# Clustered attention and two MLPs on one core: centroids by one transfer, and the inputs of two later head pairs loaded ahead

## The chip, the core and the metric

The kernel runs on one core of a Trainium2 chip. A core has a matrix engine (TensorE, PE in the views, with its weight loads PEld), three engines for elementwise work (VectorE, DVE; ScalarE, ACT; GpSimd, POOL) and a queue engine (SyncE, SP) that issues most transfers; ACT can issue transfers too. Each engine works through its own list in order and waits for the others by semaphores. Data lies in HBM, is moved by 16 DMA engines into on-chip memory (SBUF), and matmuls write to PSUM, of which a bank holds 512 numbers in each of 128 partitions. The metric is the time of one execution on the device in microseconds (us); three runs are compared by their median.

## The reference

```python
q_n = q / (norm(q) + 1e-6); k_n = k / (norm(k) + 1e-6); c_n = centroids / (norm(centroids) + 1e-6)
q_assign = argmax(q_n @ c_n.T); k_assign = argmax(k_n @ c_n.T)          # one of 16 clusters per head
scores = where(q_assign == k_assign, q @ k.T / sqrt(64), -1e9)
attn = softmax(scores); x = attn @ v                                    # B 2, heads 8, S 768, D 64
h = x @ w_in;  x = (h * sigmoid(h)) @ w_out                             # 512 -> 2048 -> 512
out = (sigmoid(x @ w_gate) * (x @ w_val)) @ w_out2                      # 512 -> 1536 -> 512
```

Only the centroids' norms change an argmax over clusters, so the kernel scales the products with a centroid by the inverse of its norm (`unit`) and leaves the norms of q and k out.

## The kernel before

Two heads make a pair, 128 partitions high (`L` is the lower half, `U` the upper); there are 8 pairs, numbered from 0. The attention runs over the pairs, each with 12 tiles of 128 queries (6 for each head, `j` 0 and 1), and then the two MLPs follow with results in `acc`, a tile of 128 x 4 x 2 x 2 x 384 numbers in SBUF that holds the attention's result: `acc[:, hp, half, b]` belongs to the pair `hp` of batch `b` and is written when that pair is finished. Before that it lies idle.

For a pair, `load` brings `qq` and `kk` (128 x 768, 384 KB each), `load_values` brings `vv`. `prep` makes what the scores need: each operand is split in a rounded part (`qh`, `kh`) and the rest (`ql`, `kl`); transfers within SBUF put `qh` and `ql` on top of each other in `qa`, and `kh` twice in `ka`; `qm` and `km` (tiles `q` and `k` in the views) hold further parts, and 16 rows each that say which cluster a query or key chose, so that the matmul itself adds the mask.

The choice of clusters: `product_of_clusters` (L157, tile `pm`, matmuls of `qq` and `kk` with the centroids `cc`), `scaled` (L277, ACT, by `unit`, into `sim`), `similarities` (L168, three transposes into `ps`), a copy back (L64), and then on VectorE the maximum (`mx` for pair 0, `mk` later), equality (`eq`), rank (`wq`), its maximum, and the one-hot rows (`oh`). Transposes (`pt`) bring these to rows, which ACT and VectorE write into `q` and `k` for pair 0; for later pairs ACT writes `rows` and four small transfers carry them.

For a tile, `scores` (L468) does four matmuls into `s`, VectorE takes the maximum `nm` (L476), ACT the exponential `e` (L481); `s` has two buffers. `transposes` turns `e` (tiles `t` and `u`), copies `ph` on ACT or VectorE, and `values` (L518) multiplies by `vv` into `v`.

Set-up (L186 to L370) and the first two tiles are written out by hand for all engines but POOL. SP loads `cr` (the centroids as rows, 128 KB; L192), then `qq` and `kk` of pair 0; ACT loads the transposed centroids into `cc` in two parts (L196), whose other places VectorE has cleared. VectorE squares and sums `cr` (L263, L266), ACT takes the root (L268), VectorE forms `unit` (L269 to L274). `warm(n)` is n matmuls on zeros that fill TensorE's idle time: 10 at the start, 1 behind `pm`, 8 behind `ps`, 5 behind the second score tile. After that TensorE's order is fixed by `one_tile`: the scores of the tile two ahead, then the transposes of the present one, and pieces of `prep` of the next pair between, by a table (PIECES). VectorE, ACT, POOL and SP follow there in an order that a planner sets from this program order. Pair 1 is loaded behind the set-up's transfers (L615), pair 2 near the end of pair 0 (L656), later pairs in the middle of the pair two before. `pm` of pairs 1 and 2 is made within `prep`, that of later pairs a pair ahead.

Of the kernel before, what the change touches and what calls it, by code (L numbers as in the profile page):

```python
# [10 lines left out]
F32 = mybir.dt.float32  # L11
# [16 lines left out]
WARM = (10, 1, 8, 5)  # L28
# [3 lines left out]
def clustered_attention_then_two_mlps(ctx, tc, qT, kT, v, cen, cenT, w1i, w1o, w2g, w2v, w2o, out):  # L32
    nc = tc.nc
# [4 lines left out]
    P = 128  # L38
# [70 lines left out]
    with ExitStack() as att:  # L109
# [23 lines left out]
        def load(p):  # L133
            b, hp = divmod(p, HP)
            qq = raw.tile([P, S], F32, tag="qq", name=f"qq{p}")
            kk = raw.tile([P, S], F32, tag="kk", name=f"kk{p}")
            with after_masks(1) if p == 2 else nullcontext():
                nc.sync.dma_start(qq, qT[b, hp])
                nc.sync.dma_start(kk, kT[b, hp])
            raws[p] = (qq, kk)  # L140
# [49 lines left out]
        act_dma = nc.scalar.dma_start  # L190
        cr = cp.tile([P, HP, D], F32, tag="cr", name="cr")
        dma(cr, cen)  # L192
        cc = cp.tile([P, HP, 2, C], F32, tag="cc", name="cc")
        nc.vector.memset(cc, 0.0)
        for j, r in enumerate((L, U)):
            act_dma(cc[r, :, j], cenT[j])  # L196
# [4 lines left out]
        dma(kk, kT[0, 0])  # L201


        wt = fin.tile([P, S], F32, tag="rb", name="wt").bitcast(BF16)[:, 0:512]
        nc.vector.memset(wt, 0.0)
        pw = ps_v.tile([P, 512], F32, tag="v", name="pw")
# [54 lines left out]

        csq = cp.tile([P, HP, D], F32, tag="csq", name="csq")
# [26 lines left out]
        for j, (r, o) in enumerate(((L, U), (U, L))):  # L289
# [3 lines left out]
            dma(qa[o, j].bitcast(F32), ql[r].bitcast(F32))  # L293
            if j:
                dma(qm[r, j].bitcast(F32), qh[r].bitcast(F32))
        dma(vv, v[0, 0])
# [85 lines left out]

        def prep(p):
# [43 lines left out]
            sg = sim.rearrange("p t n j c -> p (t n j) c")  # L427
# [777 lines left out]
```

## Time and profile before

| | |
|---|---|
| median of 3 runs | 771.74 us (771.61 to 771.96) |
| profiled execution, span from first to last instruction | 770.1 us |
| TensorE busy | 760.9 us, 99% |
| VectorE busy | 620.1 us, 81% |
| ACT busy | 403.4 us, 52% |
| POOL busy | 393.8 us, 51% |
| bytes moved by DMA | 71.61 MB |

The page states no other time for the profiled execution than its span; the runs lie 1.6 us above it. The busy shares are means over the whole span, and say little of the first 15 us, which the change is about. A stretch there is read from the timeline: each line is an instruction or several alike, with its start, how long it ran, and in brackets how long its engine stood idle before it and what ended the wait.

### The profile page before, as it was taken

The numbers are of one execution on the slowest core, as the hardware profiler recorded it, in microseconds if no ns is written. First come the engines' busy times: TensorE is split into PE (matmuls) and PEld (weight loads), VectorE is DVE, ScalarE is ACT, GpSimd is POOL, SyncE is SP. The second block draws the span as 40 slices with busy tenths as digits, with TensorE's granted clock in tenths as the row PEclk, the third lists the DMA queues.
The fourth block names the chain that finished last, engine by engine and source line by source line (L and its number), as shares of the span: only waits on it lengthen the run. The fifth ranks groups of instructions, "written<-read, shape, count | busy, mean of one in ns | idle before, by whom it ended". The sixth has DMA issues, their size and how long they took to land.

```text
span 770.1 us, 11463 instructions
## 1 busy us (share of the span) xinstructions
PE 760.9 (99%) x4314; PEld 652.6 (85%) x4314; DVE 620.1 (81%) x787; ACT 403.4 (52%) x691; POOL 393.8 (51%) x345
## 2 busy tenths in 40 slices
PE   8999999999999999999999999999999999999998
PEld 4766777677768998998989989998998989899896
DVE  6887887788787968798978669996596997979645
ACT  6777776777886672543524516546442425344120
POOL 5235134643655773476646525644573937748320
PEclk9999999999999999999999999999999999999999
DMA  7677457447122122132222111221111221121004
GB/s 207 167 210 194 113 147 195 120 125 201 32 76 83 55 82 85 53 110 82 89 77 83 55 54 60 93 69 56 40 70 55 83 83 55 55 83 55 1 0 164
DMA packets 25488, 71.61 MB, mean 93 GB/s; under 512 B 4484, under 2 KB 4952, under 8 KB 25432
## 3 DMA queue, kind: packets, MB, share of 16 engines
q1 hardware_dynamic: 24888, 70.84, 31.1%
q8 instruction: 34, 0.56, 0.3%
q14 instruction: 22, 0.18, 0.1%
q10 hardware_dynamic: 544, 0.03, 0.0%
HBM read 48.01 MB, written 3.19 MB: 66 GB/s over the span
## 4 chain that ended last, share of the span: by engine, by line
PE 92%; DVE 3%; ACT 2%; DMA 1%; issue 1%; POOL 0%; SPq 0%; ACTq 0%
PE z L1021 13%; PE s L468 8%; PE v L518 7%; PE t L505 5%; PE y L962 4%; PE h_0w L846 4%; PE h_0x L846 4%; PE g_0w L846 3%; PE g_0x L846 3%; PE v_0w L846 3%; PE v_0x L846 3%; PE r L912 2%; PE q L912 2%; PE y_00None L962 2%; PE y_20None L962 2%; PE y_11None L962 2%
## 5 line engine op out<-in xcount | busy, mean ns | idle before, releaser
L481 ACT ACTIVATE e<-s,nm 128x768 f32<-128x768 f32 x96 | 86.5, 901 | 33.8 <-DVE nm L476 32.7
L476 DVE TENSOR_REDUCE nm<-s 128x1 f32<-128x768 f32 x96 | 91.4, 953 | 10.3 <-PE s L468 8.6
L1021 PE MATMUL z<-wu,ghb 128*128 128x512 f32 (+1 forms) x292 | 89.5, 388 | 0.0
L518 PE MATMUL v<-ph,vv 128*64 128x384 f32 x384 | 69.0, 494 | 0.2 <-DVE xf L530 0.2
L1021 PEld LDWEIGHTS z<-wu,ghb 128*128 128x128 f32 x292 | 54.2, 188 | 11.7 <-ACT ghb L64 0.6
L468 PE MATMUL s<-ka,qa 128*128 128x384 f32 x192 | 57.5, 380 | 1.7 <-ACT e L481 1.3
L505 PE MATMUL t<-ident,e 128*128 128x128 f32 x384 | 58.4, 275 | 0.1
L1021 PE MATMUL z<-wu,glb 128*128 128x512 f32 (+1 forms) x146 | 56.9, 390 | 0.0
L505 PEld LDWEIGHTS t<-ident,e 128*128 128x128 f32 x384 | 44.9, 140 | 11.3 <-issue 9.0
L518 PEld LDWEIGHTS v<-ph,vv 128*64 128x64 f32 x384 | 24.7, 136 | 32.8 <-issue 29.0
L468 PE MATMUL s<-k,q 128*128 128x384 f32 x192 | 49.7, 339 | 0.0
L942 DVE TENSOR_TENSOR acc<-z,acc 128x1024 f32<-128x1024 f32 (+2 forms) x32 | 36.6, 1152 | 13.8 <-PE z L1021 13.2
L64 ACT ACTIVATE ph<-t 128x512 f32<-128x512 f32 x68 | 40.6, 598 | 12.4 <-PE t L505 11.9
L67 DVE COPY ph<-u 128x512 f32<-128x512 f32 x48 | 32.8, 682 | 16.3 <-PE u L495 16.3
L549 POOL TENSOR_TENSOR acc<-xf,rb 128x768 f32<-128x768 f32 x7 | 12.9, 1837 | 58.5 <-DMA rb<-d_rb 40.0
L741 POOL TENSOR_TENSOR wo<-co,wo 128x512 fp32r<-128x512 f32 x16 | 23.5, 1471 | 33.6 <-ACT wo L64 33.6
L468 PEld LDWEIGHTS s<-k,q 128*128 128x128 f32 x192 | 34.5, 188 | 0.5 <-ACT k L338 0.3
L468 PEld LDWEIGHTS s<-ka,qa 128*128 128x128 f32 x192 | 28.9, 190 | 6.9 <-ACT e L481 6.0
L1021 PEld LDWEIGHTS z<-wu,glb 128*128 128x128 f32 x146 | 27.4, 188 | 6.9 <-DVE glb L902 1.4
L962 PE MATMUL y<-gha,wo 128*128 128x384 f32 x128 | 32.8, 334 | 0.0
L530 DVE TENSOR_TENSOR xf<-v,other 64x384 f32<-64x384 f32 x32 | 17.7, 553 | 14.8 <-ACT other L527 14.3
L395 POOL TENSOR_SCALAR qq<-qq 128x768 f32<-128x768 f32 x7 | 5.9, 838 | 38.2 <-PE pm L157 22.3
(629 smaller groups left out, 2160.3 us busy)
## 6 DMA issues: line engine op xcount, KB each, us to landing
ri<-in_w1i SPq DMA_DIRECT2D x16, 512.0 KB, 3.2
ro<-in_w1o SPq DMA_DIRECT2D x16, 512.0 KB, 3.2
ka<-kh SPq DMA_DIRECT2D x32, 192.0 KB, 3.4
rg<-in_w2g SPq DMA_DIRECT2D x12, 512.0 KB, 3.2
rv<-in_w2v SPq DMA_DIRECT2D x12, 512.0 KB, 3.2
ru<-in_w2o SPq DMA_DIRECT2D x12, 512.0 KB, 3.2
qq<-in_qT SPq DMA_DIRECT2D x8, 384.0 KB, 3.7
kk<-in_kT SPq DMA_DIRECT2D x8, 384.0 KB, 4.3
```

Of the source, the lines that this page charges most:

```text
L64: return nc.scalar.activation(o, i, AF.Copy)
L67: return nc.vector.tensor_copy(o, i)
L468: nc.tensor.matmul(s[:, g, 0:HS], lhsT=a[:, j, i * P : (i + 1) * P], rhs=c[:, j, g * HS : (g + 1) * HS], start=n == 0, stop=n == 1,)
L476: maxima.append(nc.vector.tensor_reduce(nm, s[:, :, 0:HS], axis=AX.XY, op=ALU.max, negate=True))
L481: x = nc.scalar.activation(e, s[:, :, 0:HS], AF.Exp, bias=nm, scale=1.0, accum_out=tots[p][:, n : n + 1])
L505: nc.tensor.transpose(t[:, kt, :], e[:, kt * P : (kt + 1) * P], ident)
L518: m = nc.tensor.matmul(o[(L, U)[kt % 2]], lhsT=vv[:, j, kt, :], rhs=ring[:, kt, g * G : (g + 1) * G], start=n < 2, stop=n >= NT - 2,)
L846: nc.tensor.matmul(o[:, b, 0:HS], lhsT=w[a][s][:, k, :], rhs=right[b, q][t][:, k, :], start=start and k == 0 and n == 0, stop=k == KQ - 1 ...
L912: nc.tensor.matmul(o[:, h, 0:HS], lhsT=w[f"a{m + 1}{r + 1}"][s][:, k, :], rhs=right[b, f"{r + 1}{h + 1}"][t][:, k, :], start=r == 0 and k ...
L942: added.append(nc.vector.tensor_tensor(z, o, z, op=ALU.add))
L962: nc.tensor.matmul(o[:, d, 0:width], lhsT=s[:, d, k, :], rhs=t[:, c], start=k == 0 and m == 0, stop=k == 1 and m == 2,)
L1021: nc.tensor.matmul(o[:, a, c], lhsT=s[:, q * P : (q + 1) * P], rhs=r[:, c], start=k == 0 and m == 0, stop=k == 1 and m == 2, skip_group_ch ...
```

## The change

The centroids. The transposed centroids come by one transfer to a tile `cs`, which two copies on VectorE bring to their places in `cc`; `cr` is loaded by ACT's queue behind it and no longer by SP's.

The loads. `qq` and `kk` of pairs 1 and 2 go into parts of `acc` that are written last in the first half of the attention. SP issues pair 1's right behind those of pair 0, and pair 2's behind the first four operand transfers, of which the last, `qa<-ql`, is now two of half the size. So `raw` gets pair 3 next.

The products. `pm` of pair 1 is made in the set-up behind `ps` of pair 0, and `pm` of pair 2 behind the second score tile, where `ps` of pair 1 now stands as well. Their scaled products lie in `acc` too. The fillers there go from 8 and 5 to 4 and 0.

```diff
-WARM = (10, 1, 8, 5)
+WARM = (10, 1, 4, 0)
+EARLY = (1, 2)
...
         act_dma = nc.scalar.dma_start
+        cs = cp.tile([P, HP, C], F32, tag="cs", name="cs")
+        act_dma(cs, cenT.rearrange("j d h c -> (j d) h c"))
         cr = cp.tile([P, HP, D], F32, tag="cr", name="cr")
-        dma(cr, cen)
+        act_dma(cr, cen)
         cc = cp.tile([P, HP, 2, C], F32, tag="cc", name="cc")
         nc.vector.memset(cc, 0.0)
-        for j, r in enumerate((L, U)):
-            act_dma(cc[r, :, j], cenT[j])
...
         dma(qq, qT[0, 0])
         dma(kk, kT[0, 0])
-
+        for p in EARLY:
+            raws[p] = tuple(acc[:, HP - p, n].rearrange("p b s -> p (b s)") for n in range(2))
+
+        def load_early(p):
+            for t, a in zip(raws[p], (qT, kT)):
+                dma(t, a[divmod(p, HP)])
+
+        load_early(EARLY[0])
...
+        for j, r in enumerate((L, U)):
+            nc.vector.tensor_copy(cc[r, :, j], cs[r])
         csq = cp.tile([P, HP, D], F32, tag="csq", name="csq")
         nc.vector.tensor_tensor(csq, cr, cr, op=ALU.mult)
...
-            dma(qa[o, j].bitcast(F32), ql[r].bitcast(F32))
+            for c in (slice(0, HS), slice(HS, S)) if j == 0 else (slice(0, S),):
+                dma(qa[o, j, c].bitcast(F32), ql[r, c].bitcast(F32))
             if j:
                 dma(qm[r, j].bitcast(F32), qh[r].bitcast(F32))
+            else:
+                load_early(EARLY[1])
         dma(vv, v[0, 0])
...
         similarities(ps, sums)
+        early = {EARLY[0]: ps_v.tile([P, 512], F32, tag="v", name=f"pm{EARLY[0]}")}
+        product_of_clusters(early[EARLY[0]], EARLY[0], *raws[EARLY[0]])
         warm(WARM[2])
...
         query_rows(0, pts[1], 0, half, half)
+        first_products = {p: acc[:, 0, n, B - 1, :] for n, p in enumerate(EARLY)}
+        scaled(EARLY[0], first_products[EARLY[0]], early[EARLY[0]][:, 0:HS])
...
-            sim = first_products.pop(p)
-            sums = sim.rearrange("p t n j c -> p (t n j c)")
-            yield
-            ps = ps_t.tile([P, 512], F32, tag="t", name=f"ps{p}")
-            similarities(ps, sums)
-            cast(nc.scalar, sums, ps[:, 0:HS])
+            sums = first_products.pop(p)
+            yield
+            if p != EARLY[0]:
+                seen(p, sums, nc.scalar)
...
-        if NPAIR > 1:
-            load(1)
-            load_values(1)
+        load_values(1)
         tiles = [(p, j, i) for p in range(NPAIR) for j in range(2) for i in range(NT)]
         for t in tiles[:2]:
             scores(*t)
+        seen(EARLY[0], first_products[EARLY[0]], nc.vector)
+        late_bank = ps_v.tile([P, 512], F32, tag="v", name=f"pm{EARLY[1]}")
+        product_of_clusters(late_bank, EARLY[1], *raws[EARLY[1]])
+        scaled(EARLY[1], first_products[EARLY[1]], late_bank[:, 0:HS])
         warm(WARM[3])
...
                 pieces(99)
-                if p == 0:
-                    load(p + 2)
                 if p + 2 < NPAIR:
                     load_values(p + 2)
```

`seen` is `similarities` and the copy back, as before. How the lists of the engines change is shown at two places.

The first is the start. SP's list before, from its first transfer (numbers in the names tell buffers apart):

```order
L192 DMA cr_105<-in_cen 128x256
L200 DMA qq0_111<-in_qT 128x768
L201 DMA kk0_112<-in_kT 128x768
L290 DMA qa0_194<-qh0_196 64x768
L291 DMA ka0_195<-kh0_198 64x768
L292 DMA ka0_195<-kh0_198 64x768
L293 DMA qa0_194<-ql0_197 64x768
L290 DMA qa0_194<-qh0_196 64x768
```

and now:

```order
L200 DMA qq0_111<-in_qT 128x768
L201 DMA kk0_112<-in_kT 128x768
L207 DMA acc_58<-in_qT 128x768
L207 DMA acc_58<-in_kT 128x768
L299 DMA qa0_198<-qh0_200 64x768
L300 DMA ka0_199<-kh0_202 64x768
L301 DMA ka0_199<-kh0_202 64x768
L303 DMA qa0_198<-ql0_201 64x384 x2
L207 DMA acc_58<-in_qT 128x768
L207 DMA acc_58<-in_kT 128x768
L299 DMA qa0_198<-qh0_200 64x768
```

ACT's list before, from its first transfer:

```order
L196 DMA cc_107<-in_cenT 64x4x16 x2
L229 ACT_TABLE_LOAD
L229 ACTIVATE sq_135<-sq_135 128x1
L267 ACTIVATE identb_134<-ident_129 128x128
L268 ACTIVATE r1_179<-r0_178 128x4
L284 ACTIVATE qh0_196<-qq0_111 128x768
L64 ACTIVATE kh0_198<-kk0_112 128x768
L277 ACTIVATE sim0_219<-pm0_213,unit_184 128x384
```

and now:

```order
L192 DMA cs_105<-in_cenT 128x64
L194 DMA cr_107<-in_cen 128x256
L236 ACT_TABLE_LOAD
L236 ACTIVATE sq_137<-sq_137 128x1
L276 ACTIVATE identb_136<-ident_131 128x128
L277 ACTIVATE r1_183<-r0_182 128x4
L293 ACTIVATE qh0_200<-qq0_111 128x768
L65 ACTIVATE kh0_202<-kk0_112 128x768
L286 ACTIVATE sim0_226<-pm0_220,unit_188 128x384
```

SP has lost `cr` and has two loads of pair 1 (into `acc`) ahead of the first operand transfer and two of pair 2 behind the fourth. ACT issues `cr` second; the root `r1<-r0`, which needs the sum of the squares of `cr`, stands ahead of `qh` as before.

The second place lies behind the first two score tiles. TensorE's list before, from the second tile to the transposes of the first:

```order
L468 MATMUL s0_0_1_283<-ka0_195,qa0_194 128x384 x2
L468 MATMUL s0_0_1_283<-k2_0_140,q2_0_138 128x384 x2
L210 LDWEIGHTS wt_116
L210 MATMUL pw_118<-wt_116 128x512
...
L468 MATMUL s0_0_2_305<-ka0_195,qa0_194 128x384 x2
L468 MATMUL s0_0_2_305<-k2_0_140,q2_0_138 128x384 x2
L505 MATMUL t0_0_0_320<-ident_129,e0_0_0_280 128x128 x4
```

and now:

```order
L486 MATMUL s0_0_1_288<-ka0_199,qa0_198 128x384 x2
L486 MATMUL s0_0_1_288<-k2_0_142,q2_0_140 128x384 x2
L168 MATMUL ps1_297<-ident_131,acc_58 128x128 x3
L157 MATMUL pm2_302<-acc_58,cc_109 32x384 x4
L486 MATMUL s0_0_2_316<-ka0_199,qa0_198 128x384 x2
L486 MATMUL s0_0_2_316<-k2_0_142,q2_0_140 128x384 x2
L523 MATMUL t0_0_0_331<-ident_131,e0_0_0_285 128x128 x4
L530 MATMUL u0_0_0_337<-ident_131,e0_0_0_285 128x128 x2
```

VectorE's list before, from the maximum of the second tile to that of the fifth:

```order
L476 TENSOR_REDUCE nm0_0_1_288<-s0_0_1_283 128x1
L173 TENSOR_REDUCE mx0_1_314<-sim0_219 128x12
L176 TENSOR_TENSOR eq0_1_316<-sim0_219,mx0_1_314 128x192
L178 TENSOR_TENSOR wq0_1_318<-eq0_1_316,rank_157 128x192
L476 TENSOR_REDUCE nm0_0_2_310<-s0_0_2_305 128x1
L181 TENSOR_REDUCE mw0_1_356<-wq0_1_318 128x12
L317 TENSOR_TENSOR oh_0_142<-wq0_1_318,mw0_1_356 128x6x16
L476 TENSOR_REDUCE nm0_0_3_334<-s0_0_3_329 128x1
L317 TENSOR_TENSOR oh_0_142<-wq0_1_318,mw0_1_356 128x6x16
L67 COPY ph_266<-u0_0_0_326 128x2x256
L67 COPY ph_266<-t0_0_1_341 128x4x128
L476 TENSOR_REDUCE nm0_0_4_352<-s0_0_4_347 128x1
```

and now:

```order
L68 COPY acc_58<-ps1_297 128x384
L176 TENSOR_TENSOR eq0_1_327<-sim0_226,mx0_1_325 128x192
L494 TENSOR_REDUCE nm0_0_2_321<-s0_0_2_316 128x1
L178 TENSOR_TENSOR wq0_1_329<-eq0_1_327,rank_159 128x192
L181 TENSOR_REDUCE mw0_1_367<-wq0_1_329 128x12
L494 TENSOR_REDUCE nm0_0_3_345<-s0_0_3_340 128x1
L68 COPY ph_275<-u0_0_0_337 128x2x256
L331 TENSOR_TENSOR oh_0_144<-wq0_1_329,mw0_1_367 128x6x16 x2
L68 COPY ph_275<-t0_0_1_352 128x4x128
L494 TENSOR_REDUCE nm0_0_4_363<-s0_0_4_358 128x1
L353 CAST k2_0_142<-pt0_1_371 16x768
L494 TENSOR_REDUCE nm0_0_5_404<-s0_0_5_399 128x1
```

TensorE has the three transposes of pair 1 and the product of pair 2 where five fillers were (one is shown). VectorE has the copy `acc<-ps1` ahead of the third tile's maximum, the step `wq0_1` behind it, and both `oh` steps behind a copy `ph`. Behind this place TensorE's list has no `pm` and no `ps` of pair 1 and no `pm` of pair 2 any more, and is otherwise as before.

## Rows read from the trace of the kernel before

**Rows 1.** Chain of waits, 0 to 70 us: start us, us, what it went through.

```profile
1.64 4.34 DMA kk<-in_kT
...
8.10 3.34 DMA qa<-ql
...
42.57 0.85 PE pm L157 x8
```

**Rows 2.** Timeline, ACT, first 14 us: start, us, instruction, tiles, idle before.

```profile
1.02 1.28 ACTq L196 DMA_DIRECT2D cc<-in_cenT  x2
...
3.94 0.19 ACT L268 ACTIVATE r<-r 128x4 f32<-128x4 f32 x1
4.86 0.84 ACT L284 ACTIVATE qh<-qq 128x768 fp32r<-128x768 f32 x1 [0.73 <-DMA qq<-in_qT]
6.00 0.84 ACT L64 ACTIVATE kh<-kk 128x768 fp32r<-128x768 f32 x1 [0.30 <-DMA kk<-in_kT]
7.22 0.58 ACT L277 ACTIVATE sim<-pm,unit 128x384 f32<-128x384 f32 x1 [0.38 <-PE pm L157]
...
12.19 0.74 ACT L328 ACTIVATE q<-pt 16x256 fp32r<-16x256 bf16 x2
```

**Rows 3.** Timeline, VectorE, set-up.

```profile
2.82 0.43 DVE L263 TENSOR_TENSOR csq<-cr 128x256 f32<-128x256 f32 x1 [0.69 <-DMA cr<-in_cen]
3.28 0.42 DVE L266 TENSOR_REDUCE r<-csq 128x4 f32<-128x256 f32 x1
...
5.18 0.18 DVE L274 RECIPROCAL unit<-r 128x4 f32<-128x4 f32 x1
5.73 0.96 DVE L285 SCALAR_TENSOR_TENSOR ql<-qq,qh 128x768 fp32r<-128x768 f32 x1 [0.38 <-ACT qh L284]
6.88 0.95 DVE L287 TENSOR_TENSOR k<-kk,kh 64x768 fp32r<-64x768 f32 x1 [0.18 <-ACT kh L64]
8.50 0.36 DVE L173 TENSOR_REDUCE mx<-ps 128x12 f32<-128x192 f32 x1 [0.67 <-PE ps L168]
```

**Rows 4.** Timeline, TensorE and its weight loads, set-up and first tiles.

```profile
6.28 0.48 PE L157 MATMUL pm<-qq,cc 128*32 128x384 f32 x1 [0.52 <-DMA cc<-in_cenT]
...
8.30 1.89 PE L210 MATMUL pw<-wt 128*128 128x512 bf16 x8
...
12.22 0.19 PEld L468 LDWEIGHTS s<-k,q 128*128 128x128 f32 x1 [0.26 <-ACT k L338]
...
12.85 0.51 PE L468 MATMUL s<-k,q 128*128 128x384 f32 x2
...
14.74 0.62 PE L468 MATMUL s<-ka,qa 128*128 128x384 f32 x2 [0.28 <-ACT e L481]
```

**Rows 5.** Stretches: us, busy of PE, PEld, DVE, ACT, POOL; PEclk, DMA share, GB/s.

```profile
3.00:5.00 2.00, 2.00 (x6) 0.76 (x5) 1.36 (x7) 1.26 (x5) 0.60 (x1) 1.00 0.99 340
15.75:24.39 8.64, 8.52 (x65) 6.75 (x64) 8.54 (x13) 7.21 (x15) 6.30 (x7) 1.00 0.74 221
24.98:33.36 8.38, 7.88 (x56) 5.46 (x58) 8.31 (x13) 6.19 (x12) 0.39 (x1) 1.00 0.90 210
36.00:62.00 26.00, 25.95 (x176) 17.79 (x174) 21.68 (x32) 18.62 (x37) 8.71 (x7) 1.00 0.71 189
```

**Rows 6.** Timeline, VectorE, the eighth tile's maximum.

```profile
24.98 0.96 DVE L476 TENSOR_REDUCE nm<-s 128x1 f32<-128x768 f32 x1 [0.59 <-PE s L468]
```

**Rows 7.** Timeline, SP's queue, its first two transfers.

```profile
0.73 0.39 SPq L192 DMA_DIRECT2D cr<-in_cen  x1
1.17 0.42 SPq L200 DMA_DIRECT2D qq<-in_qT  x1
```

**Rows 8.** DMA queues, 1.5 to 3.6 us: packets, MB, share of engines.

```profile
q1 hardware_dynamic: 245, 0.44, 80.3%
```

**Rows 9.** DMA queues, 4.6 to 5.7 us: q1 is SP's, q10 ACT's.

```profile
q1 hardware_dynamic: 53, 0.11, 26.3%
q10 hardware_dynamic: 283, 0.02, 17.5%
```

More of the change, by code (lines that the diff above doesn't have):

```diff
@@ L136, in load @@
             kk = raw.tile([P, S], F32, tag="kk", name=f"kk{p}")
-            with after_masks(1) if p == 2 else nullcontext():
-                nc.sync.dma_start(qq, qT[b, hp])
-                nc.sync.dma_start(kk, kT[b, hp])
+            nc.sync.dma_start(qq, qT[b, hp])
+            nc.sync.dma_start(kk, kT[b, hp])
             raws[p] = (qq, kk)
@@ L201, in clustered_attention_then_two_mlps @@
         dma(kk, kT[0, 0])
+        for p in EARLY:
[4 more added lines that the diff above has]
+        load_early(EARLY[0])
         wt = fin.tile([P, S], F32, tag="rb", name="wt").bitcast(BF16)[:, 0:512]
         nc.vector.memset(wt, 0.0)
-        pw = ps_v.tile([P, 512], F32, tag="v", name="pw")
+        pw = ps_s.tile([P, 512], F32, tag="s", name="pw")
         def warm(n):
@@ L370, in clustered_attention_then_two_mlps, with seen @@
         query_rows(0, pts[1], 0, half, half)
+        first_products = {p: acc[:, 0, n, B - 1, :] for n, p in enumerate(EARLY)}
+        scaled(EARLY[0], first_products[EARLY[0]], early[EARLY[0]][:, 0:HS])
         on_pool = {}
-        first_products = {}
         def clusters(p):
-            sim = wk.tile([P, NT, 2, 2, C], F32, tag="sim", name=f"sim{p}", bufs=1)
+            sim = wk.tile([P, HS], F32, tag="sim", name=f"sim{p}", bufs=1)
             pm = ps_t.tile([P, 512], F32, tag="t", name=f"pm{p}")
             product_of_clusters(pm, p, *raws[p][:2])
-            scaled(p, sim.rearrange("p t n j c -> p (t n j c)"), pm[:, 0:HS])
+            scaled(p, sim, pm[:, 0:HS])
             first_products[p] = sim
+        def seen(p, sums, eng):
+            ps = ps_t.tile([P, 512], F32, tag="t", name=f"ps{p}")
+            similarities(ps, sums)
+            cast(eng, sums, ps[:, 0:HS])
         def prep(p):
@@ L426, in prep @@
             W = 4 * NT
-            sg = sim.rearrange("p t n j c -> p (t n j) c")
+            sg = sums.rearrange("p (w c) -> p w c", c=C)
             queued(one, nc.vector.tensor_reduce, mk[:, 0, :], sg, axis=AX.X, op=ALU.max)
```

## The prediction

> **What bounds the kernel now.** I read the chain of waits from its start, then the timeline of each engine up to the first scores, the DMA queues in short stretches, and last the busy time by stretches. The reader should look for three things.
>
> First, the set-up is a chain, not a busy engine. The first keys land at 5.98 (1.64 + 4.34), and the copy of the low query half that the first scores need lands at 11.44 (8.10 + 3.34) [rows 1]. Close beside runs a second path, the choice of clusters: ACT turns pair 0 to `qh` and `kh` (4.86, 6.00) and scales the cluster product (`sim`, 7.22) [rows 2], VectorE picks the maximum (`mx`, 8.50) [rows 3]. The first score tile waits for both: the copy is there at 11.44, and the weights of the tile's last product wait 0.26 us for ACT's key rows `k`, the end of the choice [rows 4]. So the choice ends last; what delays it delays all that follows.
>
> Second, in the attention's first pair VectorE is the bound, although TensorE reads as busy: from 15.75 to 24.39 VectorE works 8.54 of 8.64 us, then after 0.59 us of waiting 8.31 of 8.38 us from 24.98 to 33.36 [rows 5, 6]. Third, from 36 to 62 TensorE works 25.95 of 26.00 us and VectorE only 21.68 [rows 5]: there a matmul that goes is time that goes.
>
> All sums are made against the profiled execution, whose span is 770.1 us. The timed runs (771.74) lie 1.6 us above it; that rest outside the span is taken as unchanged. Between changes of less than 0.2% (1.5 us) a measurement of this kernel does not tell.
>
> **The change part by part.**
>
> *Centroid rows `cr` to ACT's queue.* This is the term with the most in it. Now `cr` is SP's first transfer, issued at 0.73 [rows 7], and VectorE starts on it (`csq`) at 2.82 [rows 3]. After the change it is the second transfer on ACT's queue, the place that the second half of `cc` has now. ACT issues its two from 1.02 to 2.30 [rows 2]. In the queues' rows the ACT queue (q10) has no packet at all from 1.5 to 3.6 us; its second batch runs in 4.6 to 5.7, where SP's queue (q1) has only its last 53 packets left [rows 8, 9]. TensorE waits for `cc` until 6.28 [rows 4], 0.3 us after the keys. So what ACT asks for second comes when SP's second load is through, though it was asked for at nearly the same time. In the new order SP's second load is still `kk`. It is issued 0.44 us earlier, since `qq` starts at 0.73 instead of 1.17 [rows 7], so `kk` lands near 5.54. `cr` is 128 KB; at the 340 GB/s of the stretch 3.0 to 5.0 [rows 5] it takes 0.38 us more on engines that finish `kk` before that. I take 5.6 for the start of `csq`, with 3.5 (2.1 us after an issue near 1.5, as `cr` took alone) and 7.9 (behind the two new loads, 768 KB at 340 GB/s) as ends; 5.6 is by far nearest to the row of `cc`.
>
> The Trainium skill, in "DMA: Bandwidth & Descriptors" (Anatomy of one DMA), counts about 2.0 us fixed plus the bytes at 436 GB/s; by that `cr` would land near 4.0 and the set-up would lose nothing. The 2.06 us of `cr` alone on SP agree with it; the 4.6 us of `cc`'s second half do not.
>
> What hangs on `cr`: `csq` to the end of its sum 0.88 us, ACT's root `r` 0.19 and two hand-overs 0.07, the short steps to `unit` 1.23 (4.13 to 5.36), then in VectorE's order `ql` 0.96 and `k` 0.95, then `mx` [rows 2, 3]: 4.2 to 4.3 us from `csq` to `mx`. With 5.6 that is `mx` at 9.9 instead of 8.50. ACT says the same: the root stands ahead of `qh` in its order, so `qh` starts at 6.7 instead of 4.86, `kh` 0.84 later, `sim` at 8.4 instead of 7.22. With `csq` at 4.3 the term is nothing, before that a gain (rival A). **Set-up: +1.3 us.**
>
> *Centroids by one transfer, then two copies on VectorE.* Two requests become one, of 32 KB; the copies stand before `csq` and cost a few tenths that lie in its wait for `cr`. That `pm` no longer waits for `cc` is worth nothing, since `sim` behind it now waits for `kh` and `unit`.
>
> *Loads of pair 1 ahead.* 768 KB between `kk` and the copies. They take 2.3 us of DMA from 5.6 on, to 7.9; the first copy can't be asked for before `qh` is done, at 7.5. They hide in the delay of `cr`. If `cr` came early, they would lie in front of the copies, whose landing (now 11.44) would stay near 11, helped by the split of `qa<-ql` in two, of which the first score needs one. The product of pair 1 on TensorE stands where 8 of the filling matmuls (1.89 us at 8.30) and idle time are [rows 4]: nothing.
>
> *Products between the first scores.* After the second score tile (12.85 + 0.51) TensorE now fills, waits and starts the third tile at 14.74 [rows 4]. There stand instead `ps` of pair 1 (0.33), which needs ACT's scaling of 0.58 behind the query rows that end at 12.93 [rows 2], and `pm` of pair 2 (0.85): 13.5 + 0.4 + 0.85 = 14.8, so the third tile is 0.1 late. Pair 2's loads would land about 15 on a clock where this place has moved by 1.3 to 15.4; no wait, but with only 0.4 us of room. On VectorE the new cast (0.5) takes the gap before the third maximum, and one step `wq` (0.3) slips behind it, into the dense stretch. So that stretch ends 0.4 later, 24.8 instead of 24.39, against the next maximum at 24.98 now [rows 6]. TensorE loses `pm` and `ps` of pair 1 here, about 1.2 us, but VectorE lets through only 0.2. **Pair 0: -0.2 us.**
>
> *Pair 1.* `pm` of pair 2 goes from a stretch where TensorE is never idle: 0.85 us in the chain [rows 1]. ACT's scaling behind it goes as well; what is next there is the maximum of the tile before, ready 0.1 to 0.2 earlier. VectorE has 4.3 us of room in 26 [rows 5], so the whole 0.85 should pass; bounds 0 and 1.1. **Pair 1: -0.85 us.** Other pairs keep their order on TensorE and VectorE: nothing.
>
> Sum: +1.3 - 0.2 - 0.85 = +0.25, taken as +0.2: span 770.3, time 771.9.
>
> **The rivals.**
>
> *A, `cr` comes early.* If the DMA engines take ACT's requests in turn with SP's as soon as they are there, `cr` lands by 4. Then the earlier `qq` and `kk` show, up to 0.6 us at `mx` (`kk` 0.44 and the wait for `cc` 0.3, less the hand-over), and the gains stand: -0.6 - 0.2 - 0.85, and up to 0.2 more in pair 0: 769.9. For it: requests of 1 KB per partition instead of 64 bytes. Against it: no packet of ACT's queue before 3.6 [rows 8]. The Trainium skill ("DMA: Bandwidth & Descriptors", Queues, rings and completion order) has each DMA engine go round the queues packet by packet, which would bring `cr` in this way; the empty stretch in q10's rows does not show it.
>
> *B, `cr` falls behind the new loads too.* ACT's second request now ends at 2.30; SP would have asked for both loads of pair 1 by 2.6. If the order is by the time at which a request is complete, a slower issue on ACT puts one load (at 2.1) or both ahead of `cr`. With both, `csq` starts at 7.9, `mx` at 12.1, +3.6 - 1.05 = +2.5: 774.2. It decides from an end of ACT's issue later than 2.5. Against it: two-dimensional requests of 128 partitions take SP 0.39 to 0.43 [rows 7], by which ACT would end near 1.9.
>
> *C, pair 1 gives nothing*, because the maximum or the exponential of the neighbouring tile ends last once `pm` is gone: +1.3 - 0.2, 772.8. For it: `pm` is followed in the chain by ACT; against it VectorE's room.
>
> *D, the clock.* The fillers fall from 8 and 5 to 4 and 0, and TensorE will stand still longer in the set-up. The granted clock is 1.00 in every row [rows 5]; no row shows it fall. At its lower level, half, a few microseconds of matmuls would double: about 775.
>
> **How the numbers follow.** Forecast 0.57, its own range 771.2 to 772.6 (`cr` landing between 5.0 and 6.2); A 0.21, B 0.09, C 0.08, D 0.05. Faster: A and the edge of the forecast, 0.23. Slower: B and D and little else, 0.15. Same: 0.62. The range 769.7 to 773.5 leaves out B, D and the best of A.
>
> **What would show it.** `csq` waiting for `cr` until 5 to 6 us, `qh` starting right after `r` and not after its load, `mx` near 9.9; q10 empty until `qq` is through; VectorE without gaps from the third maximum to the eighth; no `pm` in pair 1 and about 0.85 less from there on. Wrong would be `csq` before 4.5, a wait of TensorE at `pm` of pair 2 for its load, a granted clock below 1.00, or a gain or loss that arises behind pair 1.

## The result: 0.9% slower, and the profile after

| | before | after |
|---|---|---|
| median of 5 runs each | 771.74 us (771.39 to 771.96) | 778.92 us (778.25 to 779.07) |
| span of the profiled execution | 770.1 us | 777.0 us |
| ratio of the times, 95% interval | | 1.009 (1.0078 to 1.0102) |

The forecast was 771.9, no change, with a range up to 773.5. The whole loss arises in the first pair of heads. The starts of VectorE's maxima `nm` in the two timelines, tile by tile from 0, show where (after minus before, us; tiles 0 to 11 belong to pair 0, 12 to 23 to pair 1):

| tile | 0 | 2 | 3 | 4 | 5 | 6 | 7 | 8 | 9 | 11 | 14 | 15 | 17 | 95 |
|---|---|---|---|---|---|---|---|---|---|---|---|---|---|---|
| | +1.29 | +2.43 | +2.54 | +5.68 | +6.86 | +6.87 | +6.36 | +6.86 | +7.72 | +7.20 | +7.49 | +6.56 | +6.92 | +6.66 |

So there are six steps: the set-up (+1.29), something ahead of tile 2 (+1.14), something ahead of tile 4 (+3.1), something ahead of tile 5 (+1.2), something ahead of tiles 8 and 9 (+1.4 together), and in pair 1 a gain at tile 15 (-0.93) between smaller losses (0.3 at tile 13, 0.4 at tile 17). The large ones are found in the timeline.

*Set-up.* VectorE and ACT of the kernel after, where [rows 2] and [rows 3] stood:

```profile
5.42 0.43 DVE L272 TENSOR_TENSOR csq<-cr 128x256 f32<-128x256 f32 x1 [0.99 <-DMA cr<-in_cen]
...
9.42 0.34 DVE L173 TENSOR_REDUCE mx<-ps 128x12 f32<-128x192 f32 x1
...
10.19 0.77 DVE L178 TENSOR_TENSOR wq<-eq,rank 128x192 bf16<-128x192 bf16 x1
```

```profile
6.34 0.20 ACT L277 ACTIVATE r<-r 128x4 f32<-128x4 f32 x1 [3.00 <-DVE r L275]
6.45 0.83 ACT L293 ACTIVATE qh<-qq 128x768 fp32r<-128x768 f32 x1
```

`cr` lands at 5.4 and ACT waits 3.00 us for the sum behind it. `mx` comes at 9.42 instead of 8.50. The step `wq` takes 0.77 us; before, the same step took 0.26 (at 9.28).

*Ahead of tile 2.* The chain of waits of the kernel after (start, us, what):

```profile
1.16 4.24 DMA cr<-in_cen
...
11.33 5.04 DMA acc<-in_kT
...
16.41 0.85 PE pm L157 x6
```

and TensorE's timeline there and behind:

```profile
15.36 0.83 PE L157 MATMUL pm<-acc,cc 128*32 128x384 f32 x2
16.41 0.85 PE L157 MATMUL pm<-acc,cc 128*32 128x384 f32 x6 [0.21 <-DMA acc<-in_kT]
17.18 0.61 PE L486 MATMUL s<-ka,qa 128*128 128x384 f32 x2
...
24.62 0.85 PE L339 MATMUL pt<-identb,oh 128*64 128x128 bf16 x6 [3.44 <-DVE oh L331]
```

The product of pair 2 waits for its second load, asked for at 11.33 and landed at 16.4. The row's idle time is only 0.21 us because two of the product's matmuls ran ahead of the load; the other six start 1.05 us behind them. The third score tile starts at 17.18 instead of 14.74 [rows 4]. Later TensorE stands still for 3.44 us, for the one-hot step `oh`.

*Ahead of tile 4.* VectorE's two `oh` steps and GpSimd at the same time:

```profile
21.18 1.61 DVE L331 TENSOR_TENSOR oh<-wq,mw 128x96 bf16<-128x96 bf16 x1
...
22.72 1.85 DVE L331 TENSOR_TENSOR oh<-wq,mw 128x96 bf16<-128x96 bf16 x1
```

```profile
20.87 1.81 POOL L420 TENSOR_TENSOR kl<-acc,kh 128x768 fp32r<-128x768 f32 x1
22.64 1.81 POOL L417 TENSOR_TENSOR ql<-acc,qh 128x768 fp32r<-128x768 f32 x1
```

Before, the two steps and the start of GpSimd's subtractions were these:

```profile
17.00 0.26 DVE L317 TENSOR_TENSOR oh<-wq,mw 128x96 bf16<-128x96 bf16 x1
...
18.05 0.25 DVE L317 TENSOR_TENSOR oh<-wq,mw 128x96 bf16<-128x96 bf16 x1
```

```profile
21.75 1.83 POOL L400 TENSOR_TENSOR kl<-kk,kh 128x768 fp32r<-128x768 f32 x1
```

Now the first ends at 22.79, 0.11 us behind the end of GpSimd's `kl` (22.68), the second at 24.57, 0.12 behind the end of `ql` (24.45). These are VectorE instructions with two operands in SBUF; before, they were over when the subtractions of pair 1 began. The `wq` of the set-up is the same: it ends at 10.96, GpSimd's scaling `acc<-acc` (10.02, 0.83) at 10.85.

*Ahead of tile 5.* The stretches, with the columns of [rows 5]:

```profile
24.50:25.00 0.50, 0.38 (x4) 0.38 (x5) 0.50 (x2) 0.00 (x0) 0.00 (x0) 0.62 1.05 209
25.00:28.00 3.00, 3.00 (x15) 2.76 (x14) 1.98 (x3) 1.92 (x5) 0.00 (x0) 0.50 1.04 222
28.00:30.00 2.00, 2.00 (x16) 1.85 (x15) 1.76 (x3) 1.10 (x3) 0.00 (x0) 0.99 1.02 246
```

After its standstill TensorE runs at the lower of its two levels (0.50, 1.2 GHz) for 3 us. From 28.5 us on it is back at 1.00.

*Ahead of tiles 8 and 9, and pair 1.* Two more steps of VectorE, of pair 1's choice of clusters, meet GpSimd's split of pair 2, which came later before (0.56 and 0.54 there):

```profile
33.37 1.06 DVE L440 TENSOR_TENSOR wq<-eq,mk 128x384 bf16<-128x384 bf16 x1
...
36.75 1.40 DVE L440 TENSOR_TENSOR oh<-wq,mk 128x384 bf16<-128x384 bf16 x1
```

The gain of 0.93 between tiles 14 and 15 is there, where `pm` of pair 2 was [rows 1], but only 0.28 of it is left at the end of pair 1.

### The profile page after: what moved, and what is told of

It reads as the page before. It is cut to its first block, busy times and chain, and to the rows that moved or that the text cites. A ratio compares the mean times of both kernels' runs of the same rounds, so it can differ in the third digit from the quotient of the medians.

```text
span 777.0 us, 11448 instructions
## 1 busy us (share of the span) xinstructions
PE 761.4 (98%) x4305; PEld 653.3 (84%) x4305; DVE 626.3 (81%) x790; ACT 402.6 (52%) x690; POOL 393.2 (51%) x345
## 4 chain that ended last, share of the span: by engine, by line
PE 91%; DVE 4%; DMA 1%; ACT 1%; issue 1%; POOL 0%; SPq 0%; ACTq 0%
PE z L1039 13%; PE s L486 8%; PE v L536 7%; PE t L523 5%; PE y L980 4%; PE h_0w L864 4%; PE h_0x L864 4%; PE g_0w L864 3%; PE g_0x L864 3%; PE v_0w L864 3%; PE v_0x L864 3%; PE r L930 2%; PE q L930 2%; PE y_00None L980 2%; PE y_11None L980 2%; PE y_10None L980 2%
## 5 line engine op out<-in xcount | busy, mean ns | idle before, releaser
L740 ACT ACTIVATE co<-ro 128x512 f32<-128x512 f32 x16 | 10.7, 672 | 25.5 <-DMA ro<-in_w1o 18.0
```

## The experiments

Theory: three things cost, `cr`'s late landing, the wait for pair 2's load, and the meeting of VectorE's two-operand steps with GpSimd's split of pair 1, which the early loads have made early; the clock falls because of the third. Rivals: the steps are slow from the DMA traffic or from their buffers; the clock falls for another reason. Ratios are to the kernel before, run on the same chip.

**pool_gate**

```diff
+            hold = sm.tile([P, 2], F32, tag="hold", name="hold", bufs=1)
+            held.append(cast(nc.gpsimd, hold, oh[0][:, 0, 1, 1, 0:2]))
...
+            with tc.issue_after(held[0].ins) if p == 1 else nullcontext():
+                nc.gpsimd.tensor_scalar(qq, qq, scale, 1.0, op0=ALU.mult, op1=ALU.mult)
...
```

> One change to the changed kernel: GpSimd copies two numbers of the one-hot rows behind the last oh step of pair 0 and starts the rest of pair 1's split (one scaling, two casts, two subtractions) only then. Theory (in the changed kernel the two oh steps at 21.18 took 3.39 us for 0.51 before because GpSimd's subtractions kl and ql ran at the same time from 20.87 to 24.45, and TensorE's wait for them let its clock fall): the oh steps take 0.25 to 0.30 each again, TensorE's wait of 3.44 at the transposes behind them falls under 0.6, the granted clock stays at 1.00 from 24 to 28. Worth 3.1 + 1.2 = 4.3 us at the seventh maximum, of which up to 1.8 may come back when the later subtractions meet VectorE's two-input steps of pair 1: 774.0 to 776.5. Rival 1 (the oh steps are slow from DMA traffic of the early loads, or from the bank or buffer they use): they stay at 1.6 each, 778.9. Rival 2 (the clock falls for another reason than the wait): oh steps short, clock still at 0.50 there, 775.7 or more.

773.67 us, ratio 1.0024 (1.0015 to 1.0033): 5.2 us of the loss of 7.2 are gone, of them 0.5 in the set-up, where `wq` takes its 0.26 again (first maximum +0.78), and 4.3 between the third and the seventh maximum. VectorE, GpSimd, and the stretch that ran at the lower clock in the kernel after:

```profile
20.96 0.42 DVE L331 TENSOR_TENSOR oh<-wq,mw 128x96 bf16<-128x96 bf16 x2
```

```profile
21.46 0.19 POOL L67 TENSOR_SCALAR hold<-oh 128x2 f32<-128x2 bf16 x1 [2.77 <-DVE oh L331]
```

```profile
25.00:28.00 3.00, 2.95 (x19) 1.73 (x19) 2.92 (x5) 2.38 (x6) 2.62 (x2) 1.00 0.97 211
```

The clock is 1.00 in every stretch from 15 to 38. With the meeting goes the fall of the clock. A little better than expected: the later meetings with the steps of pair 1 did not come.

**cr_on_sp**

```diff
-        act_dma(cr, cen)
+        dma(cr, cen)
```

> One change to the changed kernel: the centroid rows cr are SP's first transfer again, ahead of qq and kk; the transposed centroids stay one transfer on ACT. Theory (set-up loses because cr lands behind kk): csq starts near 2.9 instead of 5.42, mx at 8.4 to 8.9 instead of 9.42, the first maximum 0.6 to 1.3 earlier than 14.00; the stall at the oh steps stays, so 777.6 to 778.4. Rival (the set-up is late from the new loads that run ahead of the operand copies, not from cr): mx early, but the first maximum no earlier than 13.7, time 778.6 to 779.2.

775.95 us with runs from 772.5 to 778.5, ratio 1.0047 (1.0031 to 1.0063), below the 777.6 to 778.4 expected. `csq` starts at 3.88, the first maximum 0.49 later than before instead of 1.29. But `kk` lands later than it did (ACT's `kh` starts at 6.69, 6.00 before). In the profiled run (776.8 us) the `oh` steps took 2.41, TensorE stood still for 2.51 for them, and the clock fell there too (0.54 from 25 to 28). That the wide spread comes from runs in which they miss GpSimd's subtractions is likely, but only this one was seen in a profile.

**fillers**

```diff
             pt = ps_t.tile([P, 1024], BF16, tag="t", name="pt0_1")
+            for _ in range(12):
+                nc.tensor.matmul(pt.bitcast(F32)[:, 0:512], lhsT=wt[:, 0:P], rhs=wt, start=True, stop=True)
```

> One change to the changed kernel: twelve matmuls on zeros, into the bank that the transposes of the one-hot rows of the second half of pair 0 fill next, stand ahead of these transposes and so in TensorE's wait for the oh steps. They compute nothing that is used. Theory (the clock falls because TensorE stands still from 21.2 to 24.6): clock 1.00 from 24 to 28, oh steps as slow as before (3.4 us for both), the difference from the kernel before at the seventh maximum 5.6 instead of 6.87, time 777.6 to 777.9. Rival (the clock falls for another reason): 0.50 for some 3 us again, 778.9 or a little above.

778.51 us, ratio 1.0092 (1.0079 to 1.0105); the profile is of a run of 780.7. The clock stays at 1.00, yet nothing is won: in this order ACT takes an exponential ahead of the query rows, and TensorE waits 1.08 for ACT. Inconclusive on the clock's price; fillers_in_order repeats it with ACT's order held.

**pm2_in_prep**

```diff
-        first_products = {p: acc[:, 0, n, B - 1, :] for n, p in enumerate(EARLY)}
+        first_products = {p: acc[:, 0, n, B - 1, :] for n, p in enumerate(EARLY[:1])}
...
-        product_of_clusters(late_bank, EARLY[1], *raws[EARLY[1]])
...
```

> One change to the changed kernel: the cluster product of pair 2 is made in the preparation of pair 2 again, a pair later; its inputs are still loaded early. Theory (TensorE waits at this product for its load before the third tile): the third maximum comes 1.1 us earlier (17.1 instead of 18.18); how much of that is left at the seventh depends on the oh steps, whose start follows GpSimd's work as well: 0 to 1.1. In pair 1 the product comes back, +0.85. Time 778.6 to 779.8. Rival (the product in the first tiles costs nothing): third maximum at 18.2, 779.8.

774.0 us, ratio 1.0032 (1.0021 to 1.0043), far below what was expected. The third tile is 1.1 earlier, and so the `oh` steps start before GpSimd's subtractions (from 21.53):

```profile
19.99 0.45 DVE L331 TENSOR_TENSOR oh<-wq,mw 128x96 bf16<-128x96 bf16 x2
```

In the kernel after they started 1.2 us later, behind the wait for pair 2's load, and met the subtractions. The delay alone is not priced by this run: GpSimd's subtractions, too, start 0.7 us later here than there, behind a wait of GpSimd's for `vv`.

**memset_split** (without the low halves of pair 1)

```diff
-            nc.gpsimd.tensor_tensor(ql, qq, qh, op=ALU.subtract)
+            def rest(lo, x, hi):
+                if p > 1:
+                    return nc.gpsimd.tensor_tensor(lo, x, hi, op=ALU.subtract)
+                for _ in range(3):
+                    o = nc.gpsimd.memset(lo.bitcast(F32), 0.0)
+                return o
+
+            rest(ql, qq, qh)
...
-            on_pool["split", p] = nc.gpsimd.tensor_tensor(kl, kk, kh, op=ALU.subtract)
+            on_pool["split", p] = rest(kl, kk, kh)
```

> One change to the changed kernel: each of GpSimd's two subtractions of pair 1's split is replaced by three clears of its result, so GpSimd is about as long busy on the same memory (3 x 0.73 us for 1.82) but reads nothing. This leaves the low halves of pair 1 out of the computation. Theory (VectorE's steps with two operands in SBUF wait for a GpSimd instruction that reads SBUF and not for one that only writes): both oh steps together under 1 us although GpSimd works all the time, TensorE's wait behind them under 0.7, clock 1.00, time 773.0 to 774.5 as where GpSimd was held back. Rival (any GpSimd instruction on SBUF holds them up until it ends): each oh step waits up to 0.73, together 1.0 to 1.7, 774.5 to 776. Rival 2 (the cause is not GpSimd but the transfers): 3.4 us, 778.9.

774.53 us, ratio 1.0035 (1.0022 to 1.0047), at the border of what the theory and its rival expect; the rows decide. VectorE and GpSimd:

```profile
21.86 0.52 DVE L331 TENSOR_TENSOR oh<-wq,mw 128x96 bf16<-128x96 bf16 x1
...
22.31 0.24 DVE L331 TENSOR_TENSOR oh<-wq,mw 128x96 bf16<-128x96 bf16 x1
```

```profile
21.43 0.85 POOL L67 TENSOR_SCALAR qh<-acc 128x768 fp32r<-128x768 f32 x1
22.21 1.55 POOL L421 MEMSET ql<- 128x768 f32 x2
```

The first step meets a cast, which reads, and ends at 22.38, 0.10 behind it. The second runs inside the clears and takes its usual 0.24. In the kernel before, `wq` at 15.21 takes its 0.26 inside a clear as well (14.89 to 15.63). So for these steps a GpSimd instruction that reads is what holds VectorE up; a clear does not. DMA engines were as busy as in the kernel after (share 0.99 from 22 to 24, 0.96 there): the traffic is not the cause.

For VectorE's copies with one operand, from SBUF to SBUF, this does not hold. Three of the clears have moved to the start of this kernel, where the two copies `cc<-cs` run, and the copies take 0.83 and 0.78 us, each ending 0.05 behind a clear. VectorE and GpSimd in memset_split, then VectorE in the kernel after:

```profile
4.14 1.62 DVE L270 COPY cc<-cs 64x64 f32<-64x64 f32 x2 [1.37 <-DMA cs<-in_cenT]
```

```profile
4.18 1.54 POOL L421 MEMSET kl<- 128x768 f32 x2
```

```profile
4.04 0.39 DVE L270 COPY cc<-cs 64x64 f32<-64x64 f32 x2 [1.92 <-DMA cs<-in_cenT]
```

This is a part of why the first maximum is 2.05 us later than in the kernel before here, against 1.29 in the kernel after; the other part is the clock in the set-up (fillers_in_order).

**before_meet**

```diff
+            with tc.issue_after(held.ins) if p == 1 else nullcontext():
...
+            held = zeros(1, 1)
+        spare = st.tile([P, S], R32, tag="kl", name="spare")
+        for _ in range(2):
+            with tc.issue_after(held.ins):
+                held = nc.gpsimd.tensor_tensor(spare, qh, kh, op=ALU.subtract)
```

> The kernel before with the suspected collision put in and nothing else: GpSimd runs two subtractions of 128 x 768 from SBUF, whose result is not used, right behind its clears, that is from about 17.0 to 20.6, and starts pair 1's split behind them. Theory (a VectorE step with two operands in SBUF ends only 0.1 us after the GpSimd instruction that it meets): the first oh step (17.00, 0.26) takes about 1.8 or the second 0.9 to 1.8, the fifth maximum 1.5 to 2.8 later; GpSimd's own split ends about 2 later and may meet the two-operand steps eq and wq of pair 1 (26.4 and 27.0) too: 773.2 to 776. Rival (the early loads or the buffers of the changed kernel make these steps slow): oh steps 0.25 as before, 771.9 to 772.4.

773.48 us, ratio 1.0020 (1.0012 to 1.0029). VectorE and GpSimd in this kernel, which has no early load at all:

```profile
16.70 0.26 DVE L317 TENSOR_TENSOR oh<-wq,mw 128x96 bf16<-128x96 bf16 x1
...
17.74 1.01 DVE L317 TENSOR_TENSOR oh<-wq,mw 128x96 bf16<-128x96 bf16 x1
```

```profile
16.74 3.79 POOL L629 TENSOR_TENSOR spare<-qh,kh 128x768 fp32r<-128x768 f32 x2
```

The first `oh` step starts 0.04 ahead of GpSimd and is not held up. The second ends at 18.75, 0.11 behind the first subtraction (18.64). The meeting alone makes the step slow, and a step that starts first is not held up. As one step and not both was held up, the fifth maximum comes only 0.8 later, against the 1.5 to 2.8 expected. The rest of the loss (0.9 at the eighth maximum) follows from GpSimd's own split, which starts 1.9 later.

**all_three**

```diff
-        act_dma(cr, cen)
+        dma(cr, cen)
...
+            hold = sm.tile([P, 2], F32, tag="hold", name="hold", bufs=1)
+            held.append(cast(nc.gpsimd, hold, oh[0][:, 0, 1, 1, 0:2]))
...
+            with tc.issue_after(held[0].ins) if p == 1 else nullcontext():
...
-        product_of_clusters(late_bank, EARLY[1], *raws[EARLY[1]])
...
+            if p == 0 and i == 8:
+                clusters(2)
             scores(*fresh)
```

> Three edits to the changed kernel: cr is SP's first transfer again; GpSimd's split of pair 1 waits for the last oh step; the product of pair 2 is made ahead of the eleventh score tile instead of behind the second. Theory (the loss is these three things and the fall of the clock that one of them brings): first maximum 0.5 later than in the kernel before (kk is still slowed by the loads of pair 1), no wait ahead of the third tile, oh steps 0.25 each, seventh to eighth maximum level with the kernel before (its TensorE wait of 0.59 takes up the 0.5), pair 1 0.9 earlier: 770.8 to 772.0. Rival (something else in the change costs too, such as more transfers at once): 772.5 or more.

771.64 us, ratio 0.9996 (0.9987 to 1.0005). With the three edits the loss is gone: the theory's three places hold all of it. (The first maximum was expected 0.5 later and came 0.07 earlier than in the kernel before: `kk` was there by 6.2.) The profile has the 0.9 of pair 1 (-0.91 at the 18th maximum), but of it 0.25 is left in the span (769.9 against 770.1): the rest goes in small steps in the last pairs and the first MLP, whose causes were not traced.

**before_early2** and **before_early2b**: the kernel before with one part of the change.

```diff
             load_values(1)
+            raws[2] = tuple(acc[:, 2, n].rearrange("p b s -> p (b s)") for n in range(2))
+            for t, x in zip(raws[2], (qT, kT)):
+                dma(t, x[divmod(2, HP)])
...
+            if p == 0 and i == 8:
+                clusters(2)
```

and, in before_early2b alone,

```diff
-            with after_masks(1) if p == 2 else nullcontext():
+            with after_masks(1) if p == 3 else nullcontext():
```

> The kernel before with one part of the change in another place: pair 2's inputs are loaded ahead into the result's memory, behind the values of pair 1, and pair 2's cluster product stands ahead of the eleventh score tile, where VectorE is the bound. Set-up and first tiles as before. Theory (the product costs 0.85 to 0.93 in pair 1, where TensorE is the bound, and nothing here): same up to the twelfth maximum, 0.9 less from the sixteenth on, 770.8 to 771.3. Rival 1 (it costs as much here): 771.9. Rival 2 (the earlier split of pair 2 on GpSimd now meets VectorE's two-operand steps of pair 1): a wait in front of nm 9 or 10, 772 to 773.5.

> The kernel before with pair 2's loads ahead and its product ahead of the eleventh score tile, as in before_early2, and one edit more: pair 3's loads wait for the transfers of pair 1's mask rows, as pair 2's loads did in the kernel before. Theory (there TensorE waited 0.40 for such a transfer behind pair 3's loads, and the twelfth to fifteenth maxima lost 0.57 of the 0.9 won): that wait is gone, 0.9 to 1.0 less from the sixteenth maximum on than at the ninth, 770.7 to 771.2. Rival (the 0.57 is lost to the order of pieces on TensorE, not to that wait): as before_early2, 771.5 to 771.9.

before_early2: 771.82 us, ratio 1.0001 (0.9992 to 1.0010), no gain. Of 0.93 at the 16th maximum, 0.57 had been lost just ahead of it, part of it in a wait of TensorE:

```profile
37.19 0.59 PE L468 MATMUL s<-k,q 128*128 128x384 f32 x2 [0.40 <-DMA k<-rows]
```

before_early2b, without that wait: 771.30 us, ratio 0.9990 (0.9980 to 0.9999). It is the fastest of all, by half of what was expected of it; the product ahead of the eleventh tile itself costs 0.25.

**all_three_b**: all_three with the same edit as before_early2b.

> The changed kernel with the three edits of all_three and the same edit more: pair 3's loads wait for the transfers of pair 1's mask rows. Theory: TensorE's wait of 0.34 for such a transfer is gone, the fourteenth maximum keeps the lead of the ninth, 770.6 to 771.2. Rival: 771.4 to 771.8, as all_three.

772.28 us, runs from 770.6 to 773.7, ratio 1.0002 (0.9993 to 1.0012): missed. Its profile loses 2.1 us up to the first maximum. ACT waits for `kk`, and then TensorE's product of pair 1, ahead of the first transposes, waits for pair 1's second load, which was asked for at 2.58 and took 8.45. The step `kh` in all_three, then in all_three_b, and the product:

```profile
6.21 0.84 ACT L65 ACTIVATE kh<-kk 128x768 fp32r<-128x768 f32 x1
```

```profile
7.43 0.84 ACT L65 ACTIVATE kh<-kk 128x768 fp32r<-128x768 f32 x1 [1.70 <-DMA kk<-in_kT]
```

```profile
11.08 0.85 PE L158 MATMUL pm<-acc,cc 128*32 128x384 f32 x6 [0.72 <-DMA acc<-in_kT]
```

SP's requests for these loads are the same in both. With pair 1's loads behind it on the queue, `kk` lands anywhere from 6.2 to 7.4.

**fillers_in_order**: fillers, with the exponential of the fifth tile issued behind ACT's copy `ph` of the third.

```diff
+            if (p, j, i) == (0, 0, 4):
+                put_off.append(exponential)
+                return
...
+                with tc.issue_after(moved[0].ins):
+                    latest[:] = [put_off.pop()()]
```

> The changed kernel with twelve matmuls on zeros in TensorE's wait for the oh steps, as in fillers, but with ACT's order held as the changed kernel has it (there the fillers had also moved an exponential ahead of the query rows, and TensorE then waited 1.08 for ACT). Theory (the clock falls because TensorE stands still from 21.2 to 24.6, and what it then does at half speed costs 1.2 behind the seventh maximum): clock 1.00 throughout, oh steps still 3.4 together, fifth to seventh maxima 5.7 to 5.9 behind the kernel before instead of 5.7 to 6.9, 777.6 to 777.9. Rival (the work at half speed was hidden, the 1.2 is something else): 778.8.

777.29 us, ratio 1.0073 (1.0060 to 1.0085). TensorE, then its stretch:

```profile
20.89 2.76 PE L361 MATMUL pt<-wt 128*128 128x512 bf16 x11
25.20 0.52 PE L339 MATMUL pt<-identb,oh 128*64 128x128 bf16 x6 [1.55 <-DVE oh L331]
```

```profile
25.00:28.00 3.00, 2.80 (x23) 2.44 (x24) 2.94 (x5) 2.13 (x5) 0.03 (x1) 1.00 1.05 230
```

The `oh` steps still take 3.67 together, but the clock is 1.00 behind them, and the fifth to seventh maxima stay level (+6.26, +6.25, +6.25), where the changed kernel loses 1.2 (+5.68, +6.86, +6.87). That is the price of the clock there. The time moved by 1.6: 1.2 from the clock and 1.0 from later places, mostly milder meetings with the steps of pair 1, less 0.6 in the set-up.

That 0.6 goes with the clock too: it was not "1.00 throughout", as expected. With the set-up of the kernel after unchanged, TensorE waits 1.94 us ahead of `ps` and then runs at 0.50 from 9.5 to 12.5, through the product of pair 1 and the four fillers:

```profile
8.81 0.58 PE L168 MATMUL ps<-ident,sim 128*128 128x128 f32 x3 [1.94 <-ACT sim L286]
```

```profile
9.50:12.50 3.00, 3.00 (x12) 0.45 (x7) 2.33 (x7) 1.98 (x3) 1.57 (x3) 0.50 0.97 203
```

```profile
9.50:12.50 3.00, 1.84 (x19) 0.73 (x11) 2.23 (x7) 1.98 (x3) 1.90 (x4) 1.00 1.01 207
```

The last row is the kernel after's, where TensorE waited 2.18 at the same place and the clock did not fall. memset_split's profile has the fall (0.52; a wait of 1.84), those of pool_gate, fillers and pm2_in_prep have not. Why it comes in some of them is open.

**before_early2c**

```diff
+            if p == 0 and i in (7, 8):
...
+                product_of_clusters(halves[0], 2, *raws[2][:2], heads_of=(i - 7,))
```

> before_early2b with pair 2's product in two halves, four matmuls ahead of the tenth score tile and four ahead of the eleventh, in the bank that the values use. Theory (in before_early2b the product in one piece ahead of the eleventh tile filled TensorE's idle 0.50 and cost the rest, 0.25 at the twelfth maximum): the twelfth maximum keeps the place of the ninth, 0.9 less from the sixteenth maximum on, 770.7 to 771.2. Rival (each half delays its own tile's maximum): 771.2 to 771.8.

771.88 us, ratio 1.0005 (0.9996 to 1.0014): missed. Each half of the product takes as long as the whole, and the tenth maximum loses 0.54 and the eleventh and twelfth 0.6 more. Four matmuls here, twice, and eight in before_early2b:

```profile
29.00 0.84 PE L157 MATMUL pm<-acc,cc 128*32 128x384 f32 x4
...
31.32 0.84 PE L157 MATMUL pm<-acc,cc 128*32 128x384 f32 x4
```

```profile
30.62 0.85 PE L157 MATMUL pm<-acc,cc 128*32 128x384 f32 x8
```

## Why the prediction was wrong

**The step that failed is "Pair 0: -0.2 us".** It measured +5.9 (+1.29 at tile 0, +7.20 at tile 11): 1.1 for the load, 3.1 for the `oh` steps, 1.2 for the clock, 1.4 for the two steps of pair 1's choice, and smaller ones, less 0.5 that the wait ahead of the eighth maximum [rows 6] took up and 0.5 at the twelfth. It failed in two places.

It put VectorE's moved steps at the durations of the trace before (0.3 for `wq`) and asked what is queued on VectorE and TensorE. It never asked what GpSimd does then. [rows 5] even show it: GpSimd is busy 6.30 of 8.64 us there. Of VectorE's steps, those with two operands in SBUF have a duration that holds only as long as GpSimd doesn't read SBUF: pool_gate, memset_split and before_meet show that from three sides. The early loads moved GpSimd's split earlier, the later set-up and the wait for pair 2's load moved the steps later, and they met. The Trainium skill, in "SBUF — State Buffer" (Who interferes with whom), states this rule: a VectorE instruction with two SBUF inputs contends with a GpSimd instruction that reads SBUF, not with one that only writes, the pair of ports is locked for the whole instruction, and who issues first decides. The rows agree in each part (0.10 to 0.12 us behind GpSimd's end for the small steps, 0.24 inside a clear, 0.26 with a start 0.04 ahead). The prediction draws on the Trainium skill's page on DMA and not on this one, whose rule spoke against the change.

And "Pair 2's loads would land about 15 ...; no wait, but with only 0.4 us of room": they landed at 16.4. SP asks for the second one at 11.33, behind the two `qa<-ql`, which the late `cr` had put off to 9.28; it took 5.04 us, where `kk` took 4.34 in the kernel before [rows 1]. Small as it was, this wait moved the `oh` steps 1.1 us towards the subtractions; without it, and with GpSimd 0.7 later as well, they missed them (pm2_in_prep).

**Rival D**, the clock, had 0.05 and came true. In the kernel after it was for another reason than given there: not fewer fillers in the set-up, but a standstill of 3.44 us in pair 0. It cost 1.2 of the 7 us (fillers_in_order), where "about 775" allows 3. But in the set-up, where the forecast looked for it, the clock fell too, in two of six profiles with TensorE's set-up of the kernel after (fillers_in_order and memset_split). The profile of the kernel after was spared it; why is open, and whether more fillers would prevent it was not tried.

**The set-up, +1.3, was right in size** (+1.29) in part by luck, and mostly right in mechanism: `csq` at 5.42 (5.6 forecast), ACT's root ahead of `qh`, `mx` at 9.42 (9.9 forecast), which is +0.9 where the forecast had +1.4. It came to the sum through 0.5 that it did not hold, the `wq` held up by GpSimd; without that, pool_gate has +0.78, and with the clock at its lower level fillers_in_order has +1.85. cr_on_sp shows that `cr` isn't all of it: the loads of pair 1 delay `kk` as well. That they "hide in the delay of `cr`" was true only as long as `cr` is late. That ACT's queue would be empty until `qq` is through was wrong. The DMA queues of the kernel after from 1.5 to 3.6 us, where [rows 8] stood, and then from 3.5 to 4.75:

```profile
q1 hardware_dynamic: 187, 0.53, 76.3%
q10 hardware_dynamic: 151, 0.04, 8.2%
```

```profile
q1 hardware_dynamic: 131, 0.36, 76.6%
q10 hardware_dynamic: 136, 0.13, 28.9%
```

ACT's queue (q10) is served beside SP's (q1), packet for packet: 136 against 131 in the second stretch. But q10's packets hold about 1 KB there and q1's nearly 3. And `cs`, asked for first, comes first: the 151 packets of the first stretch hold under 300 bytes each, and a row of `cs` has 256 bytes, one of `cr` 1 KB. So `cr` comes 4.24 us after it was asked for. It lands at 5.4, about when TensorE starts on `kk` (5.27): the place that the forecast gave it, but by turns and not behind an empty queue. Counted in packets, this agrees with the packet-by-packet turns of the Trainium skill ("DMA: Bandwidth & Descriptors", Queues, rings and completion order); the early `cr` that rival A drew from them did not come, as it took neither `cs` nor the size of the packets into account. The sum of 2.0 us and the bytes at 436 GB/s, which the prediction takes from the same page of the Trainium skill, is given there for transfers that GpSimd issues; for `cr` on ACT's queue it was too short by about 2 us.

**Pair 1, -0.85, was right** where it was looked for (-0.93 at the 16th maximum, -0.92 in all_three). It came with a price that was not in the sum: pair 3's loads, freed by the change, run ahead of the mask rows, and TensorE waits for `k<-rows`. With that and a loss of 0.36 at the 18th maximum that was not traced, pair 1 as a whole gives 0.28.

## What to carry to other kernels

Before a step of VectorE or GpSimd is moved, lay the two engines' timelines side by side: a VectorE step of 0.25 us with two operands in SBUF may last as long as the GpSimd instruction that it meets, if that reads, and a load that comes earlier moves GpSimd's work too. Put such steps where GpSimd clears or is idle (but not VectorE's copies from SBUF to SBUF where it clears), or hold GpSimd back by a wait, as pool_gate does at no cost that shows. And a wait is priced with what it pushes behind it: with 1.1 us for a load the seventh maximum is 5.3 later than without (+6.87, +1.55 in pm2_in_prep).

## What was not expected of the hardware

- GpSimd's one-operand casts and scalings (0.84 us) hold VectorE up as its subtractions do: `wq` took 0.59 (memset_split) and 0.77 (the kernel after) for 0.26.
- GpSimd's clears let VectorE's steps with two operands through, but hold up its copies with one operand from SBUF to SBUF: 0.83 and 0.78 for 0.19 (memset_split).
- A transfer lands later with others queued behind it on the same queue: `kk`, asked for at 1.63 or 1.64 us, was there at 5.6 to 6.0 in five profiles (the kernel before and its variants), and at 6.2, 6.7 and 7.4 in three with 768 KB behind it.
- The cluster product's matmuls of 32 columns run side by side: eight in 0.85 us, four of one head in 0.84.
- TensorE's clock kept its higher level through a wait of 4.3 us that eleven filling matmuls shared, with 1.55 us of standstill behind them, and fell to the lower one for about 3 us behind bare waits of 3.44 and of 2.51 (cr_on_sp). In the set-up it fell behind waits of 1.94 and 1.84 and not behind one of 2.18.
